# Converting the weights with one VectorE step per chunk, the sign taken on GpSimd

## The chip, the core and the metric

The kernel runs on one core of a Trainium2 chip. The metric is the device time of one execution in microseconds; the time of a version is the median over its runs. Each engine of the core (TensorE for matrix products, VectorE, ScalarE, GpSimd, and SyncE, which here only issues transfers) works through its own list of instructions in order. Between engines there are only semaphores: an instruction that waits holds up everything behind it on its engine.

## The reference

Attention that keeps the 32 largest scores of each row, then a feed-forward layer with a hard-swish gate:

```python
scores = scale * np.matmul(q, k.transpose(0, 1, 3, 2))     # 8 batches, 8 heads, 576 x 576
kth = np.partition(scores, -32, axis=-1)[..., -32:-31]
attn = softmax(np.where(scores >= kth, scores, -1e9))      # written out with EPS in the sum
x = np.matmul(attn, v)                                     # rearranged to 4608 x 512
h = x @ w_in                                               # w_in 512 x 2048
g = h * np.clip(h + 3.0, 0.0, 6.0) / 6.0
out = g @ w_out                                            # w_out 2048 x 512
```

q, k and v come as 32-bit floats, the two weight matrices as 64-bit floats. The kernel therefore has to turn every weight from 64 to 32 bits itself, out of its two 32-bit words.

## The kernel before

**Attention.** Two heads make a `Pair`, two pairs with the same tile of 128 queries make a `Duo`. The main loop (line 608) runs over the duos, and for each over eight slots. In a slot VectorE does one of four rounds of the selection for one of the two pairs (`top`, line 276): eight maxima of each row with MAX8 (line 283), then MATCH_REPLACE8 (line 287), which takes these out, except in the fourth round. Four slots are thus one pair. After its fourth round follow, at slots that the tables in lines 570 to 583 set: `shift` (GpSimd, lines 296 and 299: from the last of the maxima), `exp` (ScalarE, lines 306, 311, 316), `inverse` (VectorE's reciprocal, line 320), `weights` (GpSimd: scale, line 330, and split into 16-bit halves, line 339), `flip` (a transpose by DMA, line 345), `join` (line 351, on ScalarE for the first two duos), `values` (TensorE, line 371) and `place` (line 381). For the first two duos the table `early` puts these closely: shift and exponentials at slot 3 or 7, the reciprocal and the weights one slot later.

**Feed-forward.** When a tile of queries is placed, a feed-forward block is queued: 64 products with `w_in` (line 398), a gate on ScalarE and GpSimd (lines 406, 408, 412, 413) and 16 products with `w_out` (line 418). `piece` takes out a few of them per slot.

**Conversion.** The weights come in 32 chunks of 128 x 512, first 16 of `w_in`, then 16 of `w_out` (lines 128 to 136). `convert` (line 96) is a generator with four stages. The first loads a chunk into a staging tile `st`, whose words alternate: `lo`, `hi`, `lo`, `hi`. The second has ScalarE make `y`, a float near 2 whose last bits are the rounded upper bits of `lo` (line 109), then write |hi| over `lo` (line 112); GpSimd clamps that to the exponents that 32 bits can hold (line 113). The third is VectorE's: shift the clamped word left by three (line 118), then take the sign bit of `hi` into `y` (line 119). In the fourth GpSimd adds the two as integers (line 124). For the first half of the chunks `y` is a PSUM tile, for the others (and there only) it is the weight's own place in SBUF. `convert_step` (line 522) runs once per slot and moves each chunk on: a chunk's clamp is issued in one slot, VectorE's step two slots later, the add one after that. On GpSimd's list a slot is therefore: add of an older chunk, clamp of a new one, and between slots the shift and the weights of attention.

The staging tiles, the transposed queries and keys, and the tiles of `flip` and `join` share one pool of 14 buffers (`kqpool`); the gate's tiles have a pool of 8 (`gpool`).

**Start.** For the first pair (lines 189 to 202) ScalarE copies the transposed keys and queries out of PSUM (lines 195, 196, 187), and `scores` with `us == (0,)` copies the first scores in three parts (lines 267 to 271).

Of the kernel before, what the change touches and what calls it, by code (L numbers as in the profile page):

```python
# [8 lines left out]
AF = mybir.ActivationFunctionType  # L9
ALU = mybir.AluOpType  # L10
F32 = mybir.dt.float32
U32 = mybir.dt.uint32
I32 = mybir.dt.int32
# [11 lines left out]
HI_LEAST = 2.0**-15  # L25
HI_MOST = 122880.0 - 2.0**-7
# [3 lines left out]
def kernel(  # L30
# [9 lines left out]
    nc = tc.nc  # L40
    P = nc.NUM_PARTITIONS
# [3 lines left out]
    JP = J * P  # L45
    R = S - JP
    NHP = H // 2
    NFC = FF // P
    assert 2 * D == P and 2 * R == P and NHP * P == DM and B % 2 == 0
    assert JP == 512 and DM == 512 and TOP_K % 8 == 0  # L50
    scale = 1.0 / float(D) ** 0.5

    def pool(name, bufs, **kw):
        return ctx.enter_context(tc.tile_pool(name=name, bufs=bufs, **kw))
# [8 lines left out]
    gpool = pool("g", 8)  # L63
# [3 lines left out]
    ps_w = pool("ps_w", 3, space=PSUM)  # L67
# [20 lines left out]
    def big():  # L88

        return ps_big.tile([P, 5 * 512], F32, tag="big", name="big")  # L90
# [2 lines left out]

    WC = 512

    def convert(dst, src, early):

        st = kqpool.tile([P, 2 * WC], U32, tag="kq", name="st")
        nc.sync.dma_start(st[:], src)
        yield
        words = st[:].rearrange("p (n two) -> p n two", two=2)
        lo, hi = words[:, :, 0], words[:, :, 1]
        y = ps_w.tile([P, WC], F32, tag="w", name="y")[:] if early else dst

        nc.scalar.activation(y, lo, AF.Copy, bias=2.0, scale=2.0**-51)

        a = lo.bitcast(F32)
        nc.scalar.activation(a, hi.bitcast(F32), AF.Abs)
        nc.gpsimd.tensor_scalar(a, a, HI_MOST, HI_LEAST, ALU.min, ALU.max)
        yield

        nc.vector.tensor_scalar(lo, lo, 3, None, ALU.logical_shift_left)
        nc.vector.scalar_tensor_tensor(  # L119
            out=dst.bitcast(U32), in0=hi, scalar=0x80000000, in1=y.bitcast(U32),  # L120
            op0=ALU.bitwise_and, op1=ALU.bitwise_or,
        )
        yield
        nc.gpsimd.tensor_tensor(
            dst.bitcast(I32), lo.bitcast(I32), dst.bitcast(I32), ALU.add
        )

    def weight_chunks():
        win, wout = moe_w_in.bitcast(U32), moe_w_out.bitcast(U32)
        for f in range(0, FF, WC):  # L130
            for g in range(NHP):
                rows = slice(g * P, (g + 1) * P)
                yield w_in[:, g, f : f + WC], win[rows, 2 * f : 2 * (f + WC)]
        for c in range(NFC):
            rows = slice(c * P, (c + 1) * P)
            yield w_out[:, c, :], wout[rows, :]
# [3 lines left out]
    class Pair:  # L140
# [31 lines left out]

        def transpose(self, first=False):

            kq = kqpool.tile([P, JP + S], F32, tag="kq", name="kq")
            self.kT, self.qT = kq[:, 0:JP], kq[:, JP : JP + S]
            c0 = 2 * JP

            def turn(ps, tiles):
                for i, j in enumerate(tiles):  # L180
                    rows = self.landed[:, j, :, :].rearrange("p h d -> p (h d)")
                    nc.tensor.transpose(ps[:, i * P : (i + 1) * P], rows, ident[:])  # L182

            def copy_left(ps):
                for hh in range(2):
                    d = slice(hh * D, (hh + 1) * D)
                    nc.scalar.copy(self.kr[d, hh, :], ps[d, 0:R])

            if first:

                ps = [ps_w.tile([P, 512], F32, tag="w", name="kqp") for _ in range(3)]
                turn(ps[0], range(J))
                turn(ps[1], [J, 2 * J])
                turn(ps[2], range(J + 1, 2 * J))
                nc.scalar.copy(self.kT, ps[0][:])
                nc.scalar.copy(kq[:, JP : JP + P], ps[1][:, 0:P])
                copy_left(ps[1][:, P:])
                self.later = [
                    (kq[:, JP + P : c0], ps[2][:, 0 : JP - P]),
                    (kq[:, c0 : c0 + R], ps[1][:, P + R : 2 * P]),  # L200
                ]
                return
            ps = big()
            turn(ps, range(2 * J + 1))
            nc.scalar.copy(kq[:, 0:c0], ps[:, 0:c0])
            nc.scalar.copy(kq[:, c0 : c0 + R], ps[:, c0 + R : c0 + 2 * R])
            copy_left(ps[:, c0:])

    class Duo:
# [15 lines left out]
        def scores(self, us=(0, 1)):  # L225

            if us[0] == 0:
                self.sc = scpool.tile([P, 2, 2 * (S + R)], F32, tag="sc", name="sc")
                self.den = mpool.tile([P, 2, 2], F32, tag="den", name="den")
            sc, nu = self.sc[:, us[0] : us[-1] + 1, :], len(us)  # L230
            ps = big()
            heads = [slice(0, D), slice(D, P)]
            qs = slice(self.qt * P, min(self.qt * P + P, S))
            banks = ps[:, 0 : 4 * 512].rearrange("p (n s) -> p n s", s=512)
            left = ps[:, 4 * 512 :]
            if self.rest:


                quarters = [
                    (i, hh, d, heads[u ^ hh])  # L240
                    for i, u in enumerate(us)
                    for hh, d in enumerate(heads)
                ]
                for i, hh, d, to in quarters:
                    pr = self.pairs[us[i]]
                    nc.tensor.matmul(banks[to, i, :], pr.qT[d, qs], pr.kT[d, :])
                for i, hh, d, to in quarters:
                    pr = self.pairs[us[i]]
                    nc.tensor.matmul(banks[to, 2 + i, 0:R], pr.qT[d, qs], pr.kr[d, hh, :])
                nc.gpsimd.memset(sc[:, :, S : S + R], 0.0)  # L250
                nc.scalar.copy(sc[:, :, 0:JP], banks[:, 0:nu, :])
                nc.scalar.copy(sc[:, :, JP:S], banks[:, 2 : 2 + nu, 0:R])
                return
            for i, u in enumerate(us):
                pr = self.pairs[u]
                nc.tensor.matmul(  # L256
                    left[:, i * P : (i + 1) * P], pr.qT[:, qs], pr.kr[:].rearrange("p h r -> p (h r)")
                )
            for i, u in enumerate(us):
                pr = self.pairs[u]  # L260
                for hh, d in enumerate(heads):
                    nc.tensor.matmul(banks[:, 2 * i + hh, :], pr.qT[d, qs], pr.kT[d, :])  # L262
            copies = [
                (sc.rearrange("p u (h s) -> p (u h) s", h=2)[:, :, 0:JP], banks[:, 0 : 2 * nu, :]),
                (sc[:, :, JP : JP + P], left[:, 0 : nu * P].rearrange("p (u r) -> p u r", r=P)),
            ]
            if us == (0,):
                (to, src), rest = copies
                copies = [rest, (to[:, 0, :], src[:, 0, :]), (to[:, 1, :], src[:, 1, :])]
            for copy in copies:  # L270
                nc.scalar.copy(*copy)  # L271

        def row(self, u, t):
            return self.sc[:, u, t * S : (t + 1) * S]
# [237 lines left out]
    chunks = list(weight_chunks())  # L512
    landing, converting, adding = [], [], []

    def land(count=1):

        for _ in range(min(count, len(chunks))):
            c = convert(*chunks.pop(0), early=len(chunks) >= NFC // 2)
            next(c)
            landing.append(c)  # L520

    def convert_step():


        for c in adding:
            next(c, None)
        adding.clear()
        if len(converting) >= 2 or not landing:
            for c in converting[:1]:
                next(c)  # L530
            adding.extend(converting[:1])
            del converting[:1]
        if landing:
            c = landing.pop(0)
            next(c)
            converting.append(c)
        land()
# [10 lines left out]
    ps = big()  # L548
    for _ in range(2):
        nc.tensor.matmul(ps[:, 0:DM], w_out[:, 0, 0:P], w_out[:, 0, :])  # L550
    first[0].load(nc.scalar)
    first[1].load()
    land()
    first[2].load()
    land()
    first[0].transpose(first=True)
    duos[0].scores((0,))
    for copy in first[0].later:
# [17 lines left out]
    early = dict(  # L576
        shift0=3, exp0=3, inverse0=4, weights0=4, flip0=5, join0=8,
        shift1=7, exp1=7, inverse1=8, weights1=8, flip1=9, join1=12, values=12, place=13,
    )
# [98 lines left out]
```

## Time and profile before

| | |
|---|---|
| time of the kernel, median of 3 runs | 1565.45 us (1564.18 to 1566.11) |
| the profiled execution | 1565.89 us, its span 1564.1 us |
| TensorE busy | 1445.2 us, 92% |
| VectorE busy | 1465.7 us, 94% |
| ScalarE busy | 1098.6 us, 70% |
| GpSimd busy | 1136.3 us, 73% |
| VectorE, line 118 | 32 instructions, 28.7 us |
| VectorE, line 119 | 32 instructions, 10.8 + 5.4 + 8.3 us |
| granted TensorE clock over the span | 0.96 |

The span is the time from the first to the last instruction of the profiled execution; the rows of the profile belong to this one execution. A row names the line, engine and operation, then output<-input. "Idle before" is the time an engine stood still ahead of an instruction, with what released it. Busy time counts an instruction from its start to its end, also where it stands started and waits for access to the memory.

### The profile page before, as it was taken

Reading aid. Unit: us, or ns where it says so; the run is one execution under the profiler, and the core shown is the slowest. Engines: PE = TensorE matmul, PEld = TensorE weight load, DVE = VectorE, ACT = ScalarE, POOL = GpSimd, SP = SyncE. Lnnn points to the kernel's source line nnn. Section 1 sums busy time; section 2 is a strip of 40 time slices with the busy share of each in tenths; the row PEclk is TensorE's granted clock in tenths of the full one; section 3 lists DMA queues with packets and bytes.
Section 4 is the critical chain, followed back from the end, with each engine's and each line's share of the span. In section 5 each row is a group of like instructions: output and inputs, shape, how many; then the busy total and the mean of one; then the engine's idle time right before and its main releaser. Section 6 shows DMA issues by size and latency. Waiting matters only on the chain.

```text
span 1564.1 us, 28780 instructions
## 1 busy us (share of the span) xinstructions
PE 1445.2 (92%) x10276; PEld 1033.0 (66%) x10276; DVE 1465.7 (94%) x3106; ACT 1098.6 (70%) x1868; POOL 1136.3 (73%) x1264
## 2 busy tenths in 40 slices
PE   5257798899999999999999999999999999999899
PEld 3143665677767777767776777677777777666675
DVE  6999999999999998999999999999999999999910
ACT  6676777677777777777777777777777777777631
POOL 3769688677777788677777778777777778777761
PEclk7568899999999999999999999999999999999999
DMA  8552445344444445355344454554344555433420
GB/s 225 160 196 57 103 83 113 74 93 81 69 83 99 98 86 108 73 100 93 76 83 85 100 96 83 89 99 98 69 83 83 99 99 92 95 68 68 79 42 14
DMA packets 450319, 144.49 MB, mean 92 GB/s; under 512 B 433280, under 2 KB 441472, under 8 KB 450176
## 3 DMA queue, kind: packets, MB, share of 16 engines
q1 hardware_dynamic: 448976, 142.36, 44.9%
q8 instruction: 81, 1.33, 0.3%
q14 instruction: 62, 0.51, 0.1%
q10 hardware_dynamic: 1200, 0.30, 0.1%
HBM read 45.09 MB, written 9.44 MB: 35 GB/s over the span
## 4 chain that ended last, share of the span: by engine, by line
DVE 42%; PE 42%; POOL 7%; ACT 4%; issue 4%; DMA 2%; SPq 1%; POOLq 0%; DVEq 0%; ACTq 0%
DVE m L283 22%; DVE wk L287 19%; PE h L398 16%; PE acc L418 15%; PE pv L371 5%; PE big L262 3%; POOL e L339 2%; POOL sc L330 1%; POOL g L413 1%; PE big L182 1%; POOL eT L351 1%; DMA t<-e 1%; PE big L256 1%; ACT sc L311 1%; ACT eT L351 1%
## 5 line engine op out<-in xcount | busy, mean ns | idle before, releaser
L283 DVE MAX8 m<-wk 128x8 f32<-128x576 f32 x864 | 614.6, 750 | 2.2
L418 PE MATMUL acc<-w_out,g 128*128 128x512 f32 x1152 | 522.1, 604 | 10.5 <-POOL g L413 10.5
L398 PEld LDWEIGHTS h<-xT,w_in 128*128 128x128 f32 x4096 | 472.1, 193 | 39.4 <-issue 21.7
L398 PE MATMUL h<-xT,w_in 128*128 128x128 f32 x4096 | 485.2, 278 | 14.0 <-ACT xT L381 13.1
L287 DVE MATCH_REPLACE8 wk<-m,wk 128x576 f32<-128x576 f32 x576 | 424.7, 746 | 0.0
L418 PEld LDWEIGHTS acc<-w_out,g 128*128 128x128 f32 x1152 | 214.1, 192 | 256.1 <-issue 234.1
L330 POOL TENSOR_SCALAR sc<-sc,den 128x576 f32<-128x576 f32 x288 | 213.0, 749 | 204.0 <-DVE den L320 177.1
L339 POOL COPY e<-sc 128x2304 uint16<-128x2304 uint16 (+1 forms) x192 | 320.0, 1677 | 10.1
L351 ACT COPY eT<-t 128x2304 uint16<-128x2304 uint16 (+1 forms) x82 | 215.9, 2633 | 57.8 <-DMA t<-e 53.5
L306 ACT ACTIVATE sc<-sc,m 128x576 f32<-128x576 f32 x288 | 210.6, 779 | 57.4 <-DVE m L283 57.0
L311 ACT ACTIVATE sc<-sc,shift 128x576 f32<-128x576 f32 x288 | 220.5, 771 | 40.9 <-POOL shift L299 38.6
L371 PE MATMUL pv<-eT,vm 128*64 128x128 f32 (+1 forms) x2560 | 163.4, 272 | 58.7 <-DVE w_out L119 20.5
L287 DVE MATCH_REPLACE8 wk<-m,sc 128x576 f32<-128x576 f32 x288 | 212.4, 746 | 0.0
L283 DVE MAX8 m<-sc 128x8 f32<-128x576 f32 x288 | 203.8, 746 | 8.9 <-ACT sc L271 8.9
L351 POOL COPY eT<-t 128x2304 uint16<-128x2304 uint16 (+1 forms) x78 | 203.5, 2609 | 7.7 <-DMA t<-e 7.7
L371 PEld LDWEIGHTS pv<-eT,vm 128*64 128x64 f32 x2560 | 134.8, 141 | 110.5 <-issue 23.8
L406 ACT ACTIVATE g<-h,three 128x512 f32<-128x512 f32 x144 | 98.8, 686 | 139.2 <-PE h L398 138.9
L413 POOL TENSOR_TENSOR g<-g,hs 128x512 f32<-128x512 f32 x144 | 184.3, 1280 | 12.2 <-POOL g L412 0.2
L271 ACT COPY sc<-big 128x256 f32<-128x256 f32 (+3 forms) x131 | 136.5, 1094 | 32.2 <-PE big L262 32.1
L412 POOL TENSOR_SCALAR g<-g 128x512 f32<-128x512 f32 x144 | 88.6, 615 | 70.4 <-ACT g L406 60.8
L262 PE MATMUL big<-kq 64*128 64x512 f32 x512 | 131.6, 633 | 0.0
L408 ACT COPY hs<-h 128x512 f32<-128x512 f32 x144 | 83.7, 581 | 0.0
(58 smaller groups left out, 1002.1 us busy)
## 6 DMA issues: line engine op xcount, KB each, us to landing
landed<-in_k_dram SPq DMA_DIRECT2D x64, 128.0 KB, 2.9
st<-in_moe_w_in_dram SPq DMA_DIRECT2D x16, 512.0 KB, 5.3
vm<-in_v_dram SPq DMA_DIRECT2D x64, 128.0 KB, 2.4
st<-in_moe_w_out_dram SPq DMA_DIRECT2D x16, 512.0 KB, 5.3
out_dram<-o SPq DMA_DIRECT2D x32, 256.0 KB, 2.5
landed<-in_q_dram SPq DMA_DIRECT2D x62, 128.0 KB, 2.9
t<-e SPq DMA_TRANSPOSE x160, 4.6
landed<-in_k_dram SPq DMA_DIRECT2D x32, 32.0 KB, 2.6
```

What stands on the lines that cost most here:

```text
L262: nc.tensor.matmul(banks[:, 2 * i + hh, :], pr.qT[d, qs], pr.kT[d, :])
L283: nc.vector.max(self.m[u][:, t, 8 * r : 8 * r + 8], self.cur[t])
L287: nc.vector.match_replace(wk, self.m[u][:, t, 8 * r : 8 * r + 8], self.cur[t], LOWEST)
L306: nc.scalar.activation(row, row, AF.Prelu, bias=m[:, t, TOP_K - 1 : TOP_K], scale=-1.0, alpha=FLAT)
L311: nc.scalar.activation(row, row, AF.Exp, bias=self.less[u][:, t : t + 1], scale=-scale / FLAT, accum_out=self.den[:, u, t : t + 1],)
L330: nc.gpsimd.tensor_scalar(row, row, self.den[:, u, t : t + 1], 1.0, ALU.mult, ALU.mult)
L339: nc.gpsimd.tensor_copy(halves[:, :, to : to + c1 - c0], words)
L351: copy(eT[:, 0 : self.nb, :] .rearrange("p c q -> p (c q)") .bitcast(U16) .rearrange("p (x h) -> p h x", h=2), self.t16[u][:, 0 : 2 * self ...
L371: nc.tensor.matmul(pv[hh * D : (hh + 1) * D, u * w : (u + 1) * w], pr.vm[:, hh, c, :] if c < J else pr.vr[:, hh, :], rhs, start=(c == 0), ...
L398: nc.tensor.matmul(h[:, (f - f0) * P : (f - f0 + 1) * P], w_in[:, i, f * P : (f + 1) * P], xT[:, i, :], start=(i == 0), stop=(i == NHP - 1),)
L413: nc.gpsimd.tensor_tensor(g[:], g[:], hs[:], ALU.mult)
L418: nc.tensor.matmul(acc[:], gs[f // nf][:, f % nf * P : (f % nf + 1) * P], w_out[:, f, :], start=(f == 0), stop=(f == NFC - 1),)
```

## The change

`y` goes straight to the weight's place in all chunks; PSUM is no longer used. |hi| goes into a tile of its own, `a`, from `gpool`, and is written first. When `lo` has been read, GpSimd writes the sign over it: (hi < 0) times -2^31, as an integer, which is the sign bit alone. VectorE then does shift and sign in one instruction: (`a` << 3) xor sign, in `a`. GpSimd's add takes `a` instead of `lo`. At the start VectorE does some of the copies for the first pair that ScalarE did: the first queries, the left-over keys, and the left-over scores.

```diff
-    def convert(dst, src, early):
+    def convert(dst, src):
...
-        y = ps_w.tile([P, WC], F32, tag="w", name="y")[:] if early else dst
-
-        nc.scalar.activation(y, lo, AF.Copy, bias=2.0, scale=2.0**-51)
-
-        a = lo.bitcast(F32)
-        nc.scalar.activation(a, hi.bitcast(F32), AF.Abs)
-        nc.gpsimd.tensor_scalar(a, a, HI_MOST, HI_LEAST, ALU.min, ALU.max)
+        a = gpool.tile([P, WC], F32, tag="g", name="a")
+        nc.scalar.activation(a[:], hi.bitcast(F32), AF.Abs)
+        nc.gpsimd.tensor_scalar(a[:], a[:], HI_MOST, HI_LEAST, ALU.min, ALU.max)
+
+        nc.scalar.activation(dst, lo, AF.Copy, bias=2.0, scale=2.0**-51)
+
+        nc.gpsimd.tensor_scalar(
+            lo.bitcast(I32), hi.bitcast(F32), 0.0, -(2.0**31), ALU.is_lt, ALU.mult
+        )
         yield
-        nc.vector.tensor_scalar(lo, lo, 3, None, ALU.logical_shift_left)
+        au = a[:].bitcast(U32)
         nc.vector.scalar_tensor_tensor(
-            out=dst.bitcast(U32), in0=hi, scalar=0x80000000, in1=y.bitcast(U32),
-            op0=ALU.bitwise_and, op1=ALU.bitwise_or,
+            out=au, in0=au, scalar=3, in1=lo,
+            op0=ALU.logical_shift_left, op1=ALU.bitwise_xor,
         )
         yield
         nc.gpsimd.tensor_tensor(
-            dst.bitcast(I32), lo.bitcast(I32), dst.bitcast(I32), ALU.add
+            dst.bitcast(I32), a[:].bitcast(I32), dst.bitcast(I32), ALU.add
         )
...
-            def copy_left(ps):
+            def copy_left(ps, copy=nc.scalar.copy):
                 for hh in range(2):
                     d = slice(hh * D, (hh + 1) * D)
-                    nc.scalar.copy(self.kr[d, hh, :], ps[d, 0:R])
+                    copy(self.kr[d, hh, :], ps[d, 0:R])
...
-                nc.scalar.copy(kq[:, JP : JP + P], ps[1][:, 0:P])
-                copy_left(ps[1][:, P:])
+                nc.vector.tensor_copy(kq[:, JP : JP + P], ps[1][:, 0:P])
+                copy_left(ps[1][:, P:], nc.vector.tensor_copy)
...
             for copy in copies:
-                nc.scalar.copy(*copy)
+                if us == (0,) and copy is rest:
+                    nc.vector.tensor_copy(*copy)
+                else:
+                    nc.scalar.copy(*copy)
...
-            c = convert(*chunks.pop(0), early=len(chunks) >= NFC // 2)
+            c = convert(*chunks.pop(0))
```

## The prediction

> **What bounds the kernel now.** I began with the engines' busy time in 20 us windows, to find the stage the change acts in. The weight conversion (lines 109 to 124, 32 chunks) runs from 12 to 148 us; nothing after that is edited. Columns: window, then busy us (and instructions) of each engine, granted TensorE clock, DMA share, GB/s.
>
> ```profile
> 40.00:60.00 20.00, 1.87 (x6) 0.29 (x2) 20.00 (x35) 14.16 (x20) 15.63 (x18) 0.50 0.62 162
> 60.00:80.00 20.00, 7.99 (x52) 5.73 (x52) 20.00 (x38) 14.10 (x24) 13.94 (x17) 0.67 0.65 189
> ```
>
> VectorE (third figure) shows no gap, GpSimd (fifth) six us of gaps, so the table says VectorE is the bound. I then read the timeline, engine by engine, and it says otherwise. From 44 to 93 us the kernel repeats every 16.15 us, once for each pair of heads (four slots). VectorE's part of one repeat (start, length, engine, line):
>
> ```profile
> 54.51 1.96 DVE L118 TENSOR_SCALAR st<-st 128x512 uint32<-128x512 uint32 x1
> 56.39 0.68 DVE L119 SCALAR_TENSOR_TENSOR w_in<-st,y 128x512 uint32<-128x512 uint32 x1
> 56.98 1.41 DVE L283 MAX8 m<-wk 128x8 f32<-128x576 f32 x2
> 58.39 1.50 DVE L118 TENSOR_SCALAR st<-st 128x512 uint32<-128x512 uint32 x1
> ```
>
> GpSimd's part of the same repeat (an idle time before an instruction and its releaser stand in brackets):
>
> ```profile
> 47.93 0.65 POOL L113 TENSOR_SCALAR st<-st 128x512 f32<-128x512 f32 x1 [1.96 <-ACT st L112]
> 51.81 0.64 POOL L113 TENSOR_SCALAR st<-st 128x512 f32<-128x512 f32 x1 [1.99 <-ACT st L112]
> 52.55 1.47 POOL L330 TENSOR_SCALAR sc<-sc,den 128x576 f32<-128x576 f32 x2
> 54.08 2.10 POOL L339 COPY e<-sc 128x2304 uint16<-128x2304 uint16 x1
> 56.15 1.46 POOL L124 TENSOR_TENSOR w_in<-st,w_in 128x512 int32<-128x512 int32 x1
> 57.70 0.65 POOL L113 TENSOR_SCALAR st<-st 128x512 f32<-128x512 f32 x1
> 58.31 1.29 POOL L124 TENSOR_TENSOR w_in<-st,w_in 128x512 int32<-128x512 int32 x1
> 59.57 0.84 POOL L113 TENSOR_SCALAR st<-st 128x512 f32<-128x512 f32 x1
> 60.38 0.18 POOL L296 TENSOR_TENSOR shift<-m 128x2 f32<-128x2 f32 x1
> ```
>
> The L118 at 54.51 takes 1.96 us where its shortest takes 0.40: it ends at 56.47, just behind the L339 copy (54.08 to 56.18). The one at 58.39 ends just behind L124. So VectorE's full bar holds 1.55 + 1.09 = 2.64 us per repeat of waiting for GpSimd's instructions: slack, not work. Next, who releases GpSimd? The shift L296 at 60.38 needs the maxima of line 283, which were done at 58.39: VectorE is two us early. ScalarE, by contrast, waits for that shift:
>
> ```profile
> 60.91 0.78 ACT L311 ACTIVATE sc<-sc,shift 128x576 f32<-128x576 f32 x1 [1.70 <-POOL shift L299]
> 63.90 2.75 ACT L351 COPY eT<-t 128x2304 uint16<-128x2304 uint16 x1
> ```
>
> and after its two exponentials, a conversion, the L351 copy and another conversion (ends 67.88) it releases GpSimd's clamp L113 at 67.96. The loop is closed without VectorE: shift, ScalarE 7.1 us, clamp 0.65, weights 1.5 + 2.1, then add, clamp, add, clamp (4.2), shift. It is the bound until 93 us. From 94 to 117 the chain of waits is ScalarE's L351 (94.44), exponentials, TensorE's L398, back to ScalarE; from 115.6 to 152 GpSimd has practically no gap, and L118 at 131.85 waits 0.83 us for a clamp. VectorE then paces the rest almost alone.
>
> **The change, part by part.** Per chunk VectorE loses L118 (32 x 0.896 = 28.7 us) and keeps one two-tensor instruction. GpSimd gains one, the sign; ScalarE swaps its two; sums go against the profiled 1564.1 us.
>
> *The one VectorE step.* Rows of the old L119:
>
> ```profile
> L119 DVE SCALAR_TENSOR_TENSOR w_in<-st,y x16: 673/676/680, 14.5 to 76.0; 128x512 uint32<-128x512 uint32 x16
> L119 DVE SCALAR_TENSOR_TENSOR w_out<-st,w_out x8: 677/1112/1783, 110.3 to 140.4; 128x512 uint32<-128x512 uint32 x8
> ```
>
> With y in PSUM it never waits (min, median, max 673/676/680 ns); with both inputs in SBUF it waits for GpSimd as L118 does. The new step has both in SBUF. At the second form's mean, 1.04 us, VectorE's bill is 28.7 + 24.5 - 33.3 = 19.9 us smaller; at 0.677 it is 31.5 smaller; at 0.677 plus L118's longest wait (1.56) it is 18 us larger. None of this reaches the end while the other loop is longer.
>
> *The sign on GpSimd.* Not in this trace. Nearest: L113, same strided words and two scalar steps, 0.65 us; far end L124, integer and two tensors, 1.30; below, 0.61 (L412). I take 0.65. It is queued before the next add, the weights and the shift, and ScalarE's exponentials, hence VectorE's reciprocal L320, wait for that shift. In each repeat two chunks stand between L339 and the shift: + 1.30. VectorE's step now waits for the sign instead of the clamp; behind it on VectorE stand the next maxima, which have the two us above.
>
> The Trainium skill (GPSIMD Engine Reference, Elementwise — side-by-side cycle accounting) gives a best case of 768 ns for 512 elements. The trace's 0.65 is less, so the trace is used; by the page each sign would cost 0.12 more and the sum below some 1.7 us more.
>
> *Abs first.* ScalarE issues Abs ahead of the copy, so the clamp starts one instruction (0.64) sooner; the sign behind it needs the copy, and ends when the clamp ended before. For the chunk in front of the weights: zero. Without that reorder it would cost 0.65 a repeat.
>
> *Turns on the shared access.* A VectorE step that runs between two GpSimd instructions delays the second. Before, L118 did that twice between L339 and the shift (1.46 for 1.29, 0.84 for 0.65): 0.18 each. The longer two-input step did it at 119.73, where L113 took 1.11: 0.46. So 2 x 0.28 = + 0.56 a repeat. Ends: no delay at all, - 0.36; three full steps of 0.68, 2.04 - 0.36 = + 1.68.
>
> So a repeat grows by 1.30 + 0.56 = 1.86 us (0.94 to 2.98). It runs three times. The stretch before it (reciprocal at 32.30 to shift at 44.22) has three unhidden signs and three turns instead of two: 1.95 + 3 x 0.28 = 2.8 (1.4 to 4.1).
>
> *VectorE's copies in the first pair.* They take 0.27 + 2 x 0.21 us off ScalarE and another 0.27 beside it: the first maxima, at 10.28, come some 0.7 sooner. ScalarE then waits for weights from HBM at 12.11, 16.56 and 22.69, and its exponentials release the reciprocal at 32.30. Cover gone, 0.7 would be gained; I take 0.
>
> *Buffers.* A staging tile is free one step earlier, so SyncE's later loads may start sooner; only three loads, all at the start, kept ScalarE waiting, so zero. Abs takes a `gpool` buffer, which an add of about eight chunks earlier frees, or a gate late in the conversion; zero while GpSimd is less than that behind, else ScalarE's exponentials would stand behind it, at most one add (1.3) each.
>
> *After 93 us.* The L351 at 94.44 waited 3.66 for L124, a staging buffer; that buffer now comes free at the VectorE step, so it waits for its transpose: L339 ends at 88.48 + 2.8 + 2 x 1.86 + about 0.4 (one turn so far) = 95.4, its transpose lands 4.6 later (page's median), and with 0.1 for the release L351 starts at 100.1: 5.7 late (shift would be 8.4 late). That lateness goes through ScalarE and L398 to the clamp at 115.59. From there GpSimd is packed: five more unhidden signs 3.25, and turns six times 0.46 against 2.2 measured, + 0.6, so its last chunk is 9.5 late. VectorE had 1.8 us of slack there (clamp done 138.3, L118 at 140.11) and needs 0.33 less; it may be passed by one add (1.29; I take half, 0.6). So the maxima at 141.04 come 9.5 - 2.1 + 0.6 = 8.0 late. The low end by the same steps: 1.4 + 2 x 0.94 puts L351 at 96.4, 2.0 late; then 3.25 - 2.2 - 2.1, in all + 1.0. The high end: 4.1 + 2 x 2.98 + 0.7 puts it at 103.9, 9.5 late; then 3.25 - 2.2 + 6 x 0.68 - 2.1 + 1.3, in all + 13.8.
>
> After that VectorE has almost no gap until 560 us, so it can't be won back. 1564.1 + 8.0 = 1572.1; the profiled run took 1.8 more than its span, and was 0.4 above the median: 1573.5.
>
> **The rivals.** (1) VectorE is the bound after all: the shift is late only because VectorE's steps hold GpSimd up, so with L118 gone it moves forward to the maxima. For it: 20.00 of 20.00, and the two instructions lengthened behind L118. Against it: they were lengthened by 0.18 each, and the shift is two us behind the maxima. It decides if VectorE, not GpSimd, is the last to be ready at the shift, which takes more than 2.0 us a repeat won by GpSimd in spite of two more signs. Then the 19.9 us come off: 1545.5. 13%. (2) Turns cost nothing and the gains at 94 us eat the rest: the low end, 1566.5, no change. 14%. (3) The sign is as slow as L124: 0.65 more on the 14 unhidden signs counted above (3 + 3 x 2 + 5) and on the five hidden behind Abs, 12 us: 1586. 7%. The forecast has 66%. That the step vanishes without effect isn't a rival: L118 is gone from VectorE's list.
>
> **How the numbers follow.** A time within 0.2% (3.1 us) can't be told from no change here. Slower: forecast and (3), 73%; same 14%; faster 13%. The range runs from just under (2) to just above the upper end, 1565 to 1580; outside lie (1) and (3), 20%.
>
> **What would show it.** GpSimd's shifts, before at 44.22, 60.38, 76.51 and 92.63, should be 18 us apart and the new VectorE step near 1.0 to 1.3 us, with VectorE now waiting openly for the sign; the first half without conversion should start near 149 instead of 141.04. Shifts 16 us apart or less would break the loop argument; a sign of 1.3 us would make (3).

## The result and the profile after

The changed kernel takes 1608.25 us (median of 5 runs, 1606.59 to 1608.55) against 1566.11 us of the kernel before (5 runs, 1564.18 to 1569.59): 1.0267 times as long, 95% interval 1.0253 to 1.0281. It is slower, as forecast, but by 42 us where 8 were forecast, and 28 us above the upper end of the range.

First, from the page of the kernel after, each engine's busy time, share and instructions; the span is 1606.8 us.

```profile
PE 1453.1 (90%) x10276; PEld 1035.9 (64%) x10276; DVE 1459.5 (91%) x3078; ACT 1096.0 (68%) x1864; POOL 1204.6 (75%) x1296
```

GpSimd is 68.3 us busier than the 1136.3 of before, for 32 more instructions: 2.1 us each. VectorE's two lines of before took 28.7 + 24.5 = 53.2 us, the one of now 42.4 us: only 10.8 less, although L118 is gone.

The 20 us windows inside the conversion, columns as in the prediction:

```profile
40.00:60.00 20.00, 4.35 (x11) 1.53 (x10) 12.53 (x24) 7.12 (x13) 18.05 (x16) 0.59 0.48 136
60.00:80.00 20.00, 2.40 (x20) 2.00 (x20) 12.75 (x21) 9.62 (x14) 19.28 (x16) 0.50 0.46 135
```

VectorE, full before, has a third of its time free; GpSimd went from 14 to 19 of 20. The view of one source line (instructions, then shortest, median and longest in ns, first and last start) gives the new sign, the clamp and VectorE's one step; the last line, from the view of waits, is the time VectorE stood for the sign (total, times, longest):

```profile
L112 POOL TENSOR_SCALAR st<-st x32: 1968/1996/2062, 14.3 to 180.6; 128x512 int32<-128x512 f32 x32
L108 POOL TENSOR_SCALAR a<-a x32: 612/936/1119, 13.6 to 179.9; 128x512 f32<-128x512 f32 x32
L120 DVE SCALAR_TENSOR_TENSOR a<-a,st x32: 674/1618/1760, 16.3 to 182.6; 128x512 uint32<-128x512 uint32 x32
DVE a L120 <- POOL st L112: 46.3, 17, 6.6
```

The sign takes 2.0 us, three times the shortest clamp (0.61) on the same number of words. GpSimd's timeline over one repeat, shift to shift (start, length, engine, line; in brackets an idle time and its releaser):

```profile
54.91 0.20 POOL L303 TENSOR_TENSOR shift<-m 128x2 f32<-128x2 f32 x1
55.20 0.69 POOL L306 TENSOR_SCALAR shift<-shift 128x2 f32<-128x2 f32 x1
55.86 1.26 POOL L125 TENSOR_TENSOR w_in<-a,w_in 128x512 int32<-128x512 int32 x1
58.41 0.61 POOL L108 TENSOR_SCALAR a<-a 128x512 f32<-128x512 f32 x1 [1.30 <-ACT a L107]
59.11 2.00 POOL L112 TENSOR_SCALAR st<-st 128x512 int32<-128x512 f32 x1
61.07 1.28 POOL L125 TENSOR_TENSOR w_in<-a,w_in 128x512 int32<-128x512 int32 x1
62.43 0.94 POOL L108 TENSOR_SCALAR a<-a 128x512 f32<-128x512 f32 x1
63.45 2.00 POOL L112 TENSOR_SCALAR st<-st 128x512 int32<-128x512 f32 x1
65.42 1.91 POOL L337 TENSOR_SCALAR sc<-sc,den 128x576 f32<-128x576 f32 x2
67.38 2.10 POOL L346 COPY e<-sc 128x2304 uint16<-128x2304 uint16 x1
...
71.50 1.97 POOL L112 TENSOR_SCALAR st<-st 128x512 int32<-128x512 f32 x1
73.43 1.26 POOL L125 TENSOR_TENSOR w_in<-a,w_in 128x512 int32<-128x512 int32 x1
74.77 0.94 POOL L108 TENSOR_SCALAR a<-a 128x512 f32<-128x512 f32 x1
75.79 1.98 POOL L112 TENSOR_SCALAR st<-st 128x512 int32<-128x512 f32 x1
77.72 0.20 POOL L303 TENSOR_TENSOR shift<-m 128x2 f32<-128x2 f32 x1
```

The repeat is 22.81 us long. One gap of 1.30 us is left; before there were two, of 1.95 and 1.96 us in the repeat from 60.38, each ahead of a clamp that waited for ScalarE:

```profile
64.09 0.65 POOL L113 TENSOR_SCALAR st<-st 128x512 f32<-128x512 f32 x1 [1.95 <-ACT st L112]
67.96 0.65 POOL L113 TENSOR_SCALAR st<-st 128x512 f32<-128x512 f32 x1 [1.96 <-ACT st L112]
```

From 58.41 on GpSimd works without a pause, so it alone is the bound; ScalarE now waits for it, in the row

```profile
78.74 0.78 ACT L318 ACTIVATE sc<-sc,shift 128x576 f32<-128x576 f32 x1 [9.88 <-POOL shift L306]
```

where the same wait was 1.70 us before. One of VectorE's steps in this repeat:

```profile
73.50 1.74 DVE L120 SCALAR_TENSOR_TENSOR a<-a,st 128x512 uint32<-128x512 uint32 x1 [5.46 <-POOL st L112]
```

The step waits 5.46 us openly, then stands started while GpSimd's add (73.43 to 74.69) runs, and does its own work behind it, to 75.24; the clamp that starts at 74.77 meanwhile takes 0.94 instead of 0.61.

How the lateness grows, read from GpSimd's shifts and from VectorE's first maxima that have no conversion around them:

| start, us | before | after | late |
|---|---|---|---|
| first reciprocal | 32.30 | 35.02 | 2.7 |
| first shift of the repeats | 44.22 | 54.91 | 10.7 |
| fourth shift | 92.63 | 123.38 | 30.8 |
| first maxima without conversion | 141.04 | 184.30 | 43.3 |
| last maxima of the kernel | 1491.37 | 1534.02 | 42.7 |
| span | 1564.1 | 1606.8 | 42.7 |

All of the loss arises before 184 us, in the conversion, and nothing of it is won back.

### The profile page after: what moved, and what is told of

Its sections match the earlier page's. It is cut to its first block, busy times and chain, and to the rows that moved or that the text cites. A ratio compares the mean times of both kernels' runs of the same rounds, so it can differ in the third digit from the quotient of the medians.

```text
span 1606.8 us, 28761 instructions
## 1 busy us (share of the span) xinstructions
PE 1453.1 (90%) x10276; PEld 1035.9 (64%) x10276; DVE 1459.5 (91%) x3078; ACT 1096.0 (68%) x1864; POOL 1204.6 (75%) x1296
## 3 DMA queue, kind: packets, MB, share of 16 engines
q8 instruction: 81, 1.33, 0.3%
## 4 chain that ended last, share of the span: by engine, by line
PE 41%; DVE 37%; POOL 13%; issue 5%; ACT 3%; DMA 1%; POOLq 0%; ACTq 0%
DVE m L290 19%; DVE wk L294 17%; PE h L405 16%; PE acc L425 15%; PE pv L378 5%; POOL st L112 3%; PE big L266 3%; POOL a L108 1%; POOL e L346 1%; POOL sc L337 1%; POOL w_in L125 1%; POOL eT L358 1%; POOL w_out L125 1%; DMA t<-e 1%; PE big L186 1%
## 5 line engine op out<-in xcount | busy, mean ns | idle before, releaser
L425 PE MATMUL acc<-w_out,g 128*128 128x512 f32 x1152 | 527.6, 609 | 24.1 <-POOL g L420 24.1
L337 POOL TENSOR_SCALAR sc<-sc,den 128x576 f32<-128x576 f32 x288 | 214.4, 754 | 200.1 <-DVE den L327 179.0
L278 ACT COPY sc<-big 128x2048 f32<-128x2048 f32 (+3 forms) x130 | 136.3, 1101 | 25.7 <-PE big L266 22.9
```

Source lines behind the costliest of these rows:

```text
L337: nc.gpsimd.tensor_scalar(row, row, self.den[:, u, t : t + 1], 1.0, ALU.mult, ALU.mult)
L425: nc.tensor.matmul(acc[:], gs[f // nf][:, f % nf * P : (f % nf + 1) * P], w_out[:, f, :], start=(f == 0), stop=(f == NFC - 1),)
```

## The experiments

Theory A, the prediction's: the conversion is bound by GpSimd and ScalarE, and the sign's time on GpSimd is the loss. Its rivals: VectorE's new step with two inputs in SBUF makes the loss (B); the moved copies, Abs first, or the buffers do (C). Each ratio below is to the kernel before as it was timed beside that run (its times lie between 1564.79 and 1567.07 us), with a 95% interval.

### The sign alone

Kernel before, with both of VectorE's steps kept; only the new GpSimd instruction is added behind each clamp, into a tile that nobody reads.

```diff
         nc.gpsimd.tensor_scalar(a, a, HI_MOST, HI_LEAST, ALU.min, ALU.max)
+        extra = gpool.tile([P, WC], F32, tag="g", name="extra")
+        nc.gpsimd.tensor_scalar(
+            extra[:].bitcast(I32), hi.bitcast(F32), 0.0, -(2.0**31), ALU.is_lt, ALU.mult
+        )
```

> The kernel before, both VectorE steps kept, with the new GpSimd instruction added behind each clamp; its result goes to a tile that nobody reads. Loop theory: three of these 2.0 us instructions stand in each repeat's loop, since Abs does not come first here: shifts 21.5 to 22.5 us apart, 1598 to 1612 us. Rival (VectorE's two-input step): VectorE's steps are as before, so 1566 to 1576.

Measured: 1608.9 us, 1.0268 times before (1.0253 to 1.0283). The group in the list of lines (busy us, mean ns, idle before):

```profile
L115 POOL TENSOR_SCALAR extra<-st 128x512 int32<-128x512 f32 x32 | 68.3, 2135 | 2.6
```

The one instruction, added alone, makes as large a loss as the whole change; the shifts are 22.56 us apart, just above the range. B and C aren't needed for a loss of this size.

### The change without the sign

Changed kernel; the sign is left out, and VectorE's step takes a column of zeros in its place.

```diff
-        nc.gpsimd.tensor_scalar(
-            lo.bitcast(I32), hi.bitcast(F32), 0.0, -(2.0**31), ALU.is_lt, ALU.mult
-        )
...
-            out=au, in0=au, scalar=3, in1=lo,
+            out=au, in0=au, scalar=3, in1=zero[:].bitcast(U32).to_broadcast([P, WC]),
```

> The changed kernel without the sign: GpSimd's instruction is left out, and VectorE's step takes a zero column from SBUF in its place, so all weights come out positive. Loop theory: the shifts stand 16.0 to 17.0 us apart and the time is 1558 to 1568 us, about that of before, although VectorE is spared one step a chunk. Rival (VectorE's two-input step): still above 1595.

Measured: 1559.75 us, 0.9957 (0.9940 to 0.9973). The shifts are 15.87 us apart, just under the range, against 16.14 before. So all the rest of the change, VectorE without L118 included, is worth 0.3 us a repeat and 7 us in all, not the 20 us that rival (1) of the prediction promised. Of B this says less than it seems to: the second input here is one column, not 512 words. The sign on ScalarE, below, decides it.

### The copies of the first pair alone

Kernel before, with nothing but VectorE's copies in the first pair.

```diff
-                nc.scalar.copy(kq[:, JP : JP + P], ps[1][:, 0:P])
-                copy_left(ps[1][:, P:])
+                nc.vector.tensor_copy(kq[:, JP : JP + P], ps[1][:, 0:P])
+                copy_left(ps[1][:, P:], nc.vector.tensor_copy)
...
-                nc.scalar.copy(*copy)
+                if us == (0,) and copy is rest:
+                    nc.vector.tensor_copy(*copy)
+                else:
+                    nc.scalar.copy(*copy)
```

> The kernel before, with only the copies of the first pair moved to VectorE. Loop theory and prediction: the first maxima some 0.5 us sooner or no sooner, hidden behind the weights' arrival; 1564.5 to 1567 us. Rival (the start is part of the loss): 1570 or more.

Measured: 1566.83 us, 1.0004 (0.9992 to 1.0016): no effect. The first maxima start at 10.24 us, 10.28 before.

### Why the sign takes 2 us: five other forms

All of these are the changed kernel with another instruction for the sign. First, floats out instead of integers and no comparison: min(hi, 0) times 0.

```diff
-            lo.bitcast(I32), hi.bitcast(F32), 0.0, -(2.0**31), ALU.is_lt, ALU.mult
+            lo.bitcast(F32), hi.bitcast(F32), 0.0, 0.0, ALU.min, ALU.mult
```

> The changed kernel, but the sign written as a float: min(hi, 0) times 0, which is minus zero or zero, with GpSimd's float output, as the clamp has it. Loop theory (GpSimd and ScalarE set the pace of the conversion, and the loss is the sign's 2.0 us): the sign takes about 0.65 us, the shifts stand 18.0 to 18.7 us apart instead of 22.8, and the time is 1572 to 1578 us. Rival (the loss is VectorE's step with two inputs in SBUF and the turns it takes): that step is unchanged, so the time stays above 1600.

Measured: 1606.12 us, 1.0253 (1.0238 to 1.0268). A miss: the sign is as slow as before, so neither the integer output nor the comparison is needed for that, and the run told nothing of A and its rivals. The view of the sign's line, and a clamp with the sign behind it:

```profile
L112 POOL TENSOR_SCALAR st<-st x32: 1966/1992/2420, 13.3 to 177.6; 128x512 f32<-128x512 f32 x32
```

```profile
79.90 0.61 POOL L108 TENSOR_SCALAR a<-a 128x512 f32<-128x512 f32 x1 [1.30 <-ACT a L107]
80.48 2.00 POOL L112 TENSOR_SCALAR st<-st 128x512 f32<-128x512 f32 x1
```

Next hi times 0 times 1, two operations of one kind (the theories A and B of its expectation are about the sign's length alone, not those above):

```diff
-            lo.bitcast(I32), hi.bitcast(F32), 0.0, -(2.0**31), ALU.is_lt, ALU.mult
+            lo.bitcast(F32), hi.bitcast(F32), 0.0, 1.0, ALU.mult, ALU.mult
```

> The changed kernel with the sign taken as hi times 0 times 1, two multiplications, again from hi into lo. Theory A (GpSimd is slow on a mixed pair of operations, as less-than and multiply or min and multiply, and quick on a pair of one kind, as min and max in the clamp or two multiplications in line 337): the sign takes 0.65 us, and by the prediction's own sum the shifts stand some 18 us apart and the time is 1569 to 1577 us. Theory B (GpSimd is slow where it reads one half of the words and writes the other): 2.0 us and 1603 to 1610.

Measured: 1570.35 us, 1.0032 (1.0021 to 1.0042). This is the prediction's own case, a sign of 0.65 us with everything else of the change kept, and the loop is as forecast:

```profile
47.26 0.20 POOL L303 TENSOR_TENSOR shift<-m 128x2 f32<-128x2 f32 x1
65.17 0.20 POOL L303 TENSOR_TENSOR shift<-m 128x2 f32<-128x2 f32 x1
83.09 0.20 POOL L303 TENSOR_TENSOR shift<-m 128x2 f32<-128x2 f32 x1
```

17.9 us apart, forecast 18.0. Then the clamp's own pair, min and max, with the smallest bounds on both sides of zero:

```diff
-            lo.bitcast(I32), hi.bitcast(F32), 0.0, -(2.0**31), ALU.is_lt, ALU.mult
+            lo.bitcast(F32), hi.bitcast(F32), 2.0**-149, -(2.0**-149), ALU.min, ALU.max
```

> The same with the clamp's pair, min and max, to plus or minus 2^-149, which keeps the sign bit and at most one last bit. Theory A: 0.65 us for the sign; theory B: 2.0 us.

A single run gave 1566.85 us, with shifts 17.55 apart. That can't be told from 1570.35, so twelve runs followed:

> The changed kernel with the clamp's pair for the sign, timed. Its single look gave 1566.85, against 1570.35 with two multiplications. Theory: GpSimd needs some 0.1 us more whenever the pair of operations changes from one instruction to the next, and with min and max behind min and max it doesn't; so 2 to 4 us under that run, 1566 to 1569, the same as the kernel before or up to 0.2% above. If the look was chance: 1569.5 to 1571.5.

Measured: 1568.75 us, 1.0018 (1.0009 to 1.0027); this interval overlaps that of the pair of products, so the time alone doesn't decide. The repeat is shorter, 17.57 us against 17.91. The sign's line, and a clamp and its sign in the timeline:

```profile
L112 POOL TENSOR_SCALAR st<-st x32: 636/654/1092, 13.1 to 143.1; 128x512 f32<-128x512 f32 x32
```

```profile
67.13 0.61 POOL L108 TENSOR_SCALAR a<-a 128x512 f32<-128x512 f32 x1 [1.30 <-ACT a L107]
67.71 0.65 POOL L112 TENSOR_SCALAR st<-st 128x512 f32<-128x512 f32 x1
```

This sign starts 0.58 us after the clamp's start, the one of after 0.70 (58.41 and 59.11 in its timeline), and so does the one with two products. But min and product, another pair than the clamp's, also starts after 0.58 us (79.90 and 80.48 above), and so do the single operations that follow. So the gap of some 0.1 us is there for two of the forms, and the theory's rule, "whenever the pair of operations changes", doesn't hold; what makes the gap isn't shown. Last, one operation alone, the comparison:

```diff
-            lo.bitcast(I32), hi.bitcast(F32), 0.0, -(2.0**31), ALU.is_lt, ALU.mult
+            lo.bitcast(F32), hi.bitcast(F32), 0.0, None, ALU.is_lt
```

> The changed kernel with the comparison alone, one operation and a float result; the weights come out wrong, since one is written instead of the sign bit. If the mixed pair is what is slow on GpSimd: 0.65 us. If the comparison by itself is slow too: 1.3 to 2.0 us.

A single run: 1590.02 us. And one product alone:

```diff
-            lo.bitcast(I32), hi.bitcast(F32), 0.0, -(2.0**31), ALU.is_lt, ALU.mult
+            lo.bitcast(F32), hi.bitcast(F32), 0.0, None, ALU.mult
```

> The changed kernel with the sign as hi times 0, one multiplication alone. If comparisons and changes of kind are slow on GpSimd, and a plain multiplication is not: 0.65 us for the sign and 1567 to 1572 us. If only a pair of operations of one kind is quick there, and everything else takes a slow way: 1.3 to 1.6 us, as the comparison alone, and 1585 to 1592 us.

A single run: 1589.45 us. The views of the sign's line with two products, with the comparison alone, and with one product alone:

```profile
L112 POOL TENSOR_SCALAR st<-st x32: 640/657/1001, 13.9 to 145.4; 128x512 f32<-128x512 f32 x32
```

```profile
L112 POOL TENSOR_SCALAR st<-st x32: 1532/1556/1589, 12.9 to 162.3; 128x512 f32<-128x512 f32 x32
```

```profile
L112 POOL TENSOR_SCALAR st<-st x32: 1533/1558/1592, 13.2 to 162.6; 128x512 f32<-128x512 f32 x32
```

The medians of this view fall into three classes: 0.65 to 0.66 us for (min, max) and (mult, mult), 1.56 for one operation alone, the comparison or the product, and 1.99 to 2.00 for (min, mult) and (is_lt, mult). What the operations compute matters less than whether the pair is one of those two; one product alone is dearer than two. Shown for these six forms; the reason isn't shown. Both (mult, mult) rows, this sign and the scaling of line 337, multiply by 1 in the second step, so the pair and that factor aren't told apart. The time follows the sign's length: 1568.75 and 1570.35, 1589.45 and 1590.02, 1606.12 and 1608.25.

### The sign on ScalarE

If GpSimd is the bound and ScalarE has room, the sign belongs there. First, hi times 0:

```diff
-        nc.gpsimd.tensor_scalar(
-            lo.bitcast(I32), hi.bitcast(F32), 0.0, -(2.0**31), ALU.is_lt, ALU.mult
-        )
+        nc.scalar.activation(lo.bitcast(F32), hi.bitcast(F32), AF.Copy, scale=0.0)
```

> The changed kernel with the sign on ScalarE (hi times 0), behind its copy; GpSimd is rid of it. Loop theory: on the way from the shift to the clamp ScalarE has as many conversions as before (Abs, copy, sign, line 351's copy, Abs), so the shifts stand 15.9 to 17 us apart and the time is 1558 to 1568 us. If ScalarE becomes the bound instead: 1572 or more.

Measured: 1562.13 us, 0.9973 (0.9959 to 0.9986), shifts 16.33 us apart. ScalarE makes a plus zero of a negative number times 0, where GpSimd's product kept the sign: in this kernel all weights come out positive, as in the one without the sign. The second form keeps the sign: negative numbers are scaled so far up that the conversion to an integer ends at the lowest one, which is the sign bit, and positive ones so far down that they become 0.

```diff
-        nc.gpsimd.tensor_scalar(
-            lo.bitcast(I32), hi.bitcast(F32), 0.0, -(2.0**31), ALU.is_lt, ALU.mult
-        )
+        nc.scalar.activation(
+            lo.bitcast(I32), hi.bitcast(F32), AF.Prelu, scale=2.0**-60, alpha=2.0**120
+        )
```

> As the run with the sign on ScalarE, but in a form that keeps it: a leaky ReLU whose slope below zero drives the result out of the 32-bit integers, so that the lowest integer, the sign bit, is written. Loop theory: one ScalarE instruction of 0.65 to 0.7 us as there, so shifts 16.0 to 16.6 us apart and 1560 to 1565 us, 0.1 to 0.4% under the kernel before. If the conversion to integers is slow on ScalarE as the sign was on GpSimd: 1575 or more.

Measured: 1560.81 us (median of 8 runs), 0.9965 (0.9953 to 0.9977): faster than the kernel after, and 0.35% under the kernel before, with an interval clear of 1. This kernel keeps VectorE's step with two inputs, the moved copies, Abs first and the buffers, so neither B nor C makes the loss. The sign's line, and GpSimd's clamps that wait for ScalarE in one repeat:

```profile
L112 ACT ACTIVATE st<-st x32: 652/682/708, 13.6 to 133.7; 128x512 int32<-128x512 f32 x32
```

```profile
63.90 0.61 POOL L108 TENSOR_SCALAR a<-a 128x512 f32<-128x512 f32 x1 [1.31 <-ACT a L107]
...
68.34 0.61 POOL L108 TENSOR_SCALAR a<-a 128x512 f32<-128x512 f32 x1 [2.59 <-ACT a L107]
```

GpSimd has 3.90 us of gaps again, as before (3.91). The repeat is 16.35 us, 0.2 longer than before: the loop gains nothing here. The gain comes later: the fourth shift is 0.9 us late (93.55), the next ones 0.4, 2.1 and 2.9 early (106.00, 127.28, 143.61 against 106.41, 129.33, 146.54), and the first maxima without conversion 3.0 early (138.01). One step of it can be read: ScalarE's join, that waited 3.66 us for an add at 94.44 in before, waits 0.67 for its transpose,

```profile
94.04 2.78 ACT L358 COPY eT<-t 128x2304 uint16<-128x2304 uint16 x1 [0.67 <-DMA t<-e]
```

since its buffer comes free at VectorE's step and no longer at the add. Which part of the rest belongs to VectorE's shorter bill wasn't separated. The other 2 of the 5 us lie behind the conversion, in code that no edit touches: from the first maxima without conversion to the last maxima of the kernel it takes 1348.5 us, 1350.3 in before (1348.3 to 1352.0 in all fourteen profiles). Why isn't shown.

### Relief for GpSimd in the kernel before

The same loop, approached from the other side: in the kernel before, the scaling of the first two duos' weights (line 330) goes to VectorE.

```diff
-                nc.gpsimd.tensor_scalar(
+                (nc.vector if self.early else nc.gpsimd).tensor_scalar(
                     row, row, self.den[:, u, t : t + 1], 1.0, ALU.mult, ALU.mult
                 )
```

> The kernel before, with line 330's scaling of the first two duos moved from GpSimd to VectorE. Loop theory (VectorE's full bar holds slack): four repeats lose 1.5 us of GpSimd's loop each, less what VectorE's new instructions hold GpSimd up, so the shifts stand 14.7 to 15.7 apart and the time falls by 2 to 6 us, to 1561 to 1565. Rival (VectorE, at 20.00 of 20.00, is the bound): eight instructions more on it, 1569 to 1575.

Measured: 1568.84 us, 1.0024 (1.0008 to 1.0039). A miss for A as I had put it, and 0.2 us short of the rival's range: with 1.5 us less on GpSimd the repeat is no shorter, but 16.56 us. The two shifts in the timeline say why:

```profile
60.95 0.29 POOL L296 TENSOR_TENSOR shift<-m 128x2 f32<-128x2 f32 x1 [2.29 <-DVE m L283]
77.55 0.29 POOL L296 TENSOR_TENSOR shift<-m 128x2 f32<-128x2 f32 x1 [2.29 <-DVE m L283]
```

GpSimd is 2.29 us early and waits for VectorE's maxima, which now stand behind the scaling:

```profile
49.05 1.82 DVE L330 TENSOR_SCALAR sc<-sc,den 128x576 f32<-128x576 f32 x2
```

So VectorE was not the bound in before, but only some two us a repeat from it, as the prediction read, and 1.82 us of scaling with its waits uses that up. Two loops of nearly the same length lie side by side there, so relief for one that burdens the other gains nothing.

## Why the prediction was off

*The failed step* is "The sign on GpSimd": "Not in this trace. Nearest: L113, same strided words and two scalar steps, 0.65 us; far end L124, integer and two tensors, 1.30 ... I take 0.65." It measured 1.99 us, outside both ends. L113 and L412 are (min, max), and the scaling L330, the only other GpSimd line with two scalar steps, is (mult, mult): the quick pairs, as the runs showed. No row held another pair, or one operation alone on as many words (line 299's single product works on two), and an add of two tensors was taken for the dearest thing GpSimd does to 512 words; nothing in the trace said so. Rival (3) had the right kind, a slow sign, and the wrong size (1.30, 1586 us). The Trainium skill (GPSIMD Engine Reference, Elementwise — side-by-side cycle accounting), with 768 ns as the best case for 512 elements, lies above the 0.65 us of the quick pairs and far below the 1.56 and 1.99 of the others.

*With the sign at the size it was given, the sum holds up to the end of the conversion.* The kernel with two products tests every other term at once:

| | forecast | sign of 0.66 us |
|---|---|---|
| repeat | 18.0 us | 17.9 us |
| first shift of the repeats, later than before | 2.8 us | 3.0 us |
| fourth shift, later than before | 8.4 us | 8.4 us |
| first maxima without conversion, later | 8.0 us | 6.7 us |
| time | 1573.5 us | 1570.35 us |
| time, above the kernel before | 8.0 us | 4.0 us |

The stretch up to the first maxima without conversion was counted 1.3 us too dear. Behind it another 2 us go (1348.3 us to the last maxima, 1350.3 in before), for which the sum has no term and the runs show no reason.

*Why 1.33 us more per sign cost 38 us more.* (1608.25 - 1570.35) / 1.33 is 28.5, nearly all of the 32 signs, where the prediction's list had 14 unhidden and, in rival (3), five hidden ones: 19 x 1.33 is only 25 us. So the sign's size was the first error, and the cover the second. The prediction hid two signs of each repeat in GpSimd's gaps of 1.95 and 1.96 us. A sign of 0.66 fits: ScalarE still releases the clamps there. One of 1.99 doesn't, and GpSimd becomes the bound of nearly the whole repeat. By the timeline above: four signs, start to next start, 1.96 + 1.97 + 1.93 + 1.93 = 7.79; less the gaps used up, 3.91 - 1.30 = 2.61; turns 0.47 (L306) + 0.33 twice (L108) + 0.44 (L337), less 0.34 in before, 1.23. Together 6.41 of the 6.68 us by which the repeat grew (22.81 against 76.51 - 60.38 = 16.13); the rest, 0.27, is of the size of the gaps of about 0.1 us that this kernel has between a clamp and its sign. The cover was named in the prediction ("zero" for the chunk in front of the weights), but not at what length of the sign it would be gone.

*The turns* were given 0.28 us each, beside the old one's 0.18, so 0.46. With the sign of 0.66 us a repeat has two, as counted, of 0.33 and 0.54 to 0.58: nearly right. With the sign of 1.99 it has four, of 0.33 to 0.47, for which the prediction had only two.

*VectorE's step* was to be near 1.0 to 1.3 us and to wait openly for the sign: median 1.62, mean 42.4 / 32 = 1.33, shortest 0.674; open waits 46.3 us in 17 places. That VectorE isn't the bound was right, shown by the kernel without the sign and by the sign alone.

*VectorE's copies* were to bring the first maxima 0.7 us forward, hidden later. No such gain can be seen: 10.62 us after and 10.24 with the copies alone, against 10.28, and over all profiles 9.94 to 12.03 with the copies moved, 10.28 to 11.73 without. ScalarE's two copies of the first scores now wait for VectorE's:

```profile
10.01 1.07 ACT L278 COPY sc<-big 128x512 f32<-128x512 f32 x2 [2.53 <-DVE sc L276]
```

So they stand behind it instead of beside it. Zero for the time was right, its reason half wrong.

*The start* was given no loss behind the weights' arrival. With signs of 2 us it has one: the first reciprocal is 2.7 us late.

*Nothing is won back* after the conversion: right within 1 us for the change, 43.3 us late at its end and 42.7 in the span; with two products 6.7 us at its end are 4.3 in the span.

## What to carry to other kernels

An instruction whose form no row of the trace shows has no upper bound by its nearest rows: on GpSimd the same 512 words took 0.65, 1.56 or 1.99 us by the operations alone, so measure the form by itself, added to the kernel before into a tile nobody reads, before the change is built on it. When a cost is called hidden, write down the length of the gap that hides it: here two gaps of two us took in a sign of 0.66, and of 2.0 almost nothing. Before work moves, look at which engine stands still in the loop that decides; here ScalarE did, and the sign costs little there (0.9965 of the time before, 0.9957 without a sign, with overlapping intervals).

## What the hardware showed unasked

- GpSimd, one scalar instruction on 128 x 512 floats: 0.65 us for (min, max), 0.66 for (mult, mult), 1.56 for is_lt or mult alone, 1.99 to 2.00 for (min, mult) and (is_lt, mult). A needless product with 1 makes one product 2.4 times as fast.
- On GpSimd a sign as (is_lt, mult) or (mult, mult) starts 0.07 to 0.09 us after the recorded end of the clamp ahead of it; as (min, max), (min, mult), is_lt alone or mult alone it starts 0.02 to 0.05 us before that end, in all 32 places of each profile. What decides isn't shown.
- ScalarE's Copy with a scale of 0 drops the sign of negative numbers; GpSimd's product with 0 keeps it. ScalarE's conversion to integers ends at the lowest integer for numbers far below it, and costs nothing extra: 0.68 us for the sign, as for Abs.
- VectorE's recorded lengths of the same MAX8 differ between profiles (mean 747 ns after, 900 in the kernel with two products) at the same pace from start to start, so that busy sums of VectorE can be compared only where these means agree, as in before (750) and after.
